# The first chunk's triangular inverse on VectorE instead of GpSimd, and the transfers of the first four chunks issued ahead of weight loads

## The chip, the cores and the metric

The kernel runs on one core of a Trainium2 chip. Its time is the device time of one execution in microseconds (us); the number that counts is the median of the runs. A core has five engines, each with an instruction queue of its own that runs in order: TensorE (PE in the profile, its weight loads PEld), VectorE (DVE), ScalarE (ACT), GpSimd (POOL) and SyncE (SP). SP and ACT also issue the DMA transfers here; a transfer that has to wait holds up everything behind it in its queue.

## What is computed

Three layers follow each other. The first is a linear recurrence over 768 time steps for 4 x 8 heads with a 40 x 40 state; the second and the third are feed-forward layers on the 3072 tokens that come out.

```python
for t in range(S):                                   # 768 steps
    y[:, :, t] = einsum('bhd,bhde->bhe', rt, state)
    Sa = einsum('bhde,bhe->bhd', state, at)
    state = state * wt[:, :, None, :] - einsum('bhd,bhe->bhde', Sa, bt) \
            + einsum('bhd,bhe->bhde', vt, kt)
...
h = x @ w_in;  x1 = (h - tanh(h)) @ w_out            # 3072 x 320, 2048 wide
...
out = sum over e of p[:, e] * (relu(x1 @ w1[e]) @ w2[e])   # 4 experts, 1024 wide
```

The weights of the second layer are 64-bit floating point numbers.

## The kernel before

**The recurrence in chunks.** Time is cut into chunks of 64 steps, and the batch into two halves, so there are 24 chunks, 12 for each half, each with 16 heads. Within a chunk the steps depend on each other through a lower triangular matrix, which is inverted in 32 x 32 blocks. A chunk goes through these stages, each a list of small steps:

- `pre`, first part (lines 262 to 277): the decay factors E are clamped and multiplied up by scans on VectorE, forward and back (L200), the keys KBT are scaled (L228), and zs is made from `a` (L217). It also issues the loads for the next chunk.
- `pre`, second part: TensorE makes the products M (L235). ScalarE copies one half of them to MB (L239), VectorE masks the other into zs (L242). `mb_out` writes MB to DRAM with four transfers in ScalarE's queue (L248). `back` turns the keys around (kbn, L257).
- `inverse` (L281 to L315): SP loads MB back as two tiles N (L288), spread so that the 128 partitions hold 16 heads' blocks, and an identity as Y (L291). Then follow 31 columns, j = 0 to 30, each with two GpSimd instructions: `tmp` is a column of Y times a row of N (L299), and Y is reduced by it (L301). Both read two tensors from SBUF and depend on the one before. SP stores Y to DRAM (L306) and reads it back as TT in another layout (L310).
- `chain` (L327): Z (L340) from the state, U = TT x Z for the first 32 steps (L349), R (L360), U for the second 32 steps, transposes T, and S, the new state. Chunk c + 1 cannot start its Z before S of chunk c.
- `post` (L408): the outputs of the chunk, SC on TensorE, which go to DRAM as xT (L441).

**Beside it: the weights of the second layer.** There are 32 blocks, up0, down0, up1 to down15. For each, SP loads a raw tile of 64-bit numbers (`raw_up`, `raw_down`, L492). The load waits for a one-element ScalarE copy from the block three before (`behind`, L174), so at most about three blocks are under way. ScalarE turns the high words into `t` (L454), VectorE decodes with four instructions (L455, L456, L458, L459), ScalarE rounds (L471), TensorE subtracts the rounded part with three matmuls ("rest", L478), and ScalarE keeps the remainder (L479). The second layer's blocks of 256 tokens (`moe1_all`) need all of that for their first round; its matmuls are "h" (L528, up) and "acc" (L591, down). Block 0 needs the outputs of chunks 0 and 1.

**What sets the order.** The steps are written in slots (`att_slot`, `spread`): slot i has the chain of chunk i, the end of the inverse of chunk i + 1, the start of that of chunk i + 2 (`INV_CUT` = 7 columns), the second part of `pre` for chunk i + 2, the first part for i + 3, and the outputs of chunk i - 1, mixed by share of the slot; weight blocks are spread over slots -0.5 to 1.75 (`share`), and the second layer begins with slot 2. A scheduler then reorders the instructions by its own estimate of when each can run, by the order of writing as priority. `soon(f)` raises a step's priority by `AHEAD` = 150 instructions. The result is one fixed order for each engine.

**Buffers.** N tiles are three: chunk c takes number 2c and 2c + 1 modulo 3, so chunk 0 has N0 and N1, chunk 1 N2 and N0, chunk 2 N1 and N2. Y and TT are two, by parity. `sc_r` is a pair of tiles that `post` uses; the first time is in chunk 0's outputs.

Of the kernel before, what the change touches and what calls it, by code (L numbers as in the profile page):

```python
# [11 lines left out]
F32 = mybir.dt.float32  # L12
# [29 lines left out]
def tile_wkv_then_moe_then_moe(ctx, tc, r, k, v, w, a, b, moe_w_in, moe_w_out, probs, w1, w2, wT, aT, rT, kbT, vP, vT, wi_in, wo_in, out):  # L42
    nc = tc.nc
# [7 lines left out]
    LAG = 1.25  # L51
    INV_CUT = 7
    AHEAD = 150
    RAW_AHEAD = 2
    CHECK_AT = 30
    NB = B // G
# [34 lines left out]
    ap2 = att.enter_context(tc.tile_pool(name="ap2", side="left", bufs=2))  # L91
# [18 lines left out]
    sc_r = [ap1.tile([128, HH // 2, C], F32, name=f"SC{i}") for i in range(2)]  # L110
# [65 lines left out]
    def soon(f):  # L176
        def g():
            with tc.high_priority(offset=AHEAD):
                f()
        return g  # L180
# [6 lines left out]
    def pre(hf, c, nxt, nxt_w):  # L187
# [57 lines left out]
        def mb_out(o):  # L245
            q = 64 * o
            for s in range(2):
                nc.scalar.dma_start(out=mt_d[c % 2][o, s].rearrange("h j t -> j h t"),  # L248
                                  in_=MB[q + 32 * s:q + 32 * s + 32, :, 32 * s:32 * s + 32])
# [16 lines left out]
        first = [clamp]  # L266
# [7 lines left out]
                first.append(lambda: [behind(zs[q:q + D, q // 64, 0, 0:1], e_r[nxt_w[1]][q:q + D, 0, 0:1]) for q in (0, 64)])  # L274
            first.append(lambda: load_w(*nxt_w, nc.scalar))
        second = [lambda g=g: m_step(g) for g in range(ng)]
        second += [lambda o=o: mb_out(o) for o in range(2)]
        second.append(back)
        return first, second

    def inverse(hf, c):  # L281
        N, Y, TT = [n_r[(2 * c + u) % 3] for u in range(2)], y_r[c % 2], tt_r[c % 2]
        X["TT", hf, c] = TT

        def load():
# [7 lines left out]
        def col(j):  # L293
            n = j // 4 + 1
            wd = 31 - j
            tmp = ap2.tile([128, 80], F32, tag="tmp", name="tmp", bufs=1)[:, 0:n * wd].rearrange("p (i t) -> p i t", i=n)
            u = j // 16
            nj = N[u][:, j - 16 * u:j - 16 * u + 1, j + 1:32]
            nc.gpsimd.tensor_tensor(out=tmp, in0=Y[:, 0:n, j:j + 1].to_broadcast([128, n, wd]),  # L299
                              in1=nj.to_broadcast([128, n, wd]), op=ALU.mult)  # L300
            nc.gpsimd.tensor_tensor(out=Y[:, 0:n, j + 1:32], in0=Y[:, 0:n, j + 1:32], in1=tmp,  # L301
                                    op=ALU.subtract)

        def store():
# [3 lines left out]
        def back():  # L308
            src = tt_d[c % 2][0]
            nc.sync.dma_start(out=TT.rearrange("p h t -> p (h t)"),  # L310
                              in_=bass.AP(src.tensor, src.offset, [[256, 4], [1024, 32], [1, 256]]))

        cols = [lambda j=j: col(j) for j in range(31)]
        return [load] + cols[:INV_CUT], cols[INV_CUT:] + [store, back]

    def start_half(hf):
        nc.gpsimd.memset(st, 0.0)
# [780 lines left out]
```

## Time and profile before

| | |
|---|---|
| median of 3 runs | 1610.53 us (1608.2 to 1612.03) |
| the profiled execution | 1613.03 us, span of its instructions 1611.3 us |
| TensorE busy | 1478.0 us, 92% of the span |
| VectorE | 807.2 us, 50% |
| ScalarE | 503.1 us, 31% |
| GpSimd | 586.7 us, 36% |
| mean granted TensorE clock | 0.948 of full speed |

The profile is one execution, taken by the hardware profiler, with the start and the duration of each instruction. An entry such as `N<-mt_d` names the output and the input of an instruction by the program's names. "Idle before" is the time in which the engine had nothing to run ahead of an instruction, and the arrow names what ended that. Rows of several like instructions are merged (x12), and the time is then the whole of them. The decode matmuls and the matmuls with 32-bit operands appear as more records than the program has instructions.

### The profile page before, as it was taken

What the parts mean: (1) busy time and instruction counts of PE and PEld (TensorE: products, weight loads), DVE (VectorE), ACT (ScalarE), POOL (GpSimd) and SP (SyncE); (2) the same over time, 40 slices, a digit from 0 to 9 for tenths busy, and PEclk for the clock granted to TensorE, in tenths of its full rate; (3) what the DMA queues carried; (4) which work ended last, traced back from release to release, by engine and by line L of the source; (5) the groups of instructions that cost most, each with busy time, mean ns of one, the idle gap of its engine ahead of it and who ended that gap; (6) DMA issues with size and microseconds to landing.
All of it is one profiled execution on the core that took longest, in us unless ns stands there. A gap on an engine that the chain in (4) does not pass through costs nothing.

```text
span 1611.3 us, 33016 instructions
## 1 busy us (share of the span) xinstructions
PE 1478.0 (92%) x13178; PEld 1330.4 (83%) x13178; DVE 807.2 (50%) x1604; ACT 503.1 (31%) x1239; POOL 586.7 (36%) x1543
## 2 busy tenths in 40 slices
PE   3587898898989899989998999999999999999998
PEld 2366698888878788879998989898898989898997
DVE  8588756665656566666556443332333333332332
ACT  3344433333333333333345462121221212121111
POOL 4888865648485484665703001000000101010000
PEclk9578799999998999999999999999999999999999
DMA  4556522332432323232215331000010101000011
GB/s 127 130 151 158 132 50 72 97 83 69 101 86 77 82 69 95 76 94 66 61 39 156 101 100 29 8 21 17 1 36 1 37 1 36 1 1 1 0 50 51
DMA packets 163938, 103.26 MB, mean 64 GB/s; under 512 B 101952, under 2 KB 139840, under 8 KB 163776
## 3 DMA queue, kind: packets, MB, share of 16 engines
q1 hardware_dynamic: 97412, 71.64, 16.1%
q10 hardware_dynamic: 66364, 29.44, 7.6%
q8 instruction: 105, 1.72, 0.4%
q14 instruction: 57, 0.47, 0.1%
HBM read 82.82 MB, written 18.22 MB: 63 GB/s over the span
## 4 chain that ended last, share of the span: by engine, by line
PE 57%; DMA 6%; POOL 5%; DVE 3%; issue 3%; ACT 1%; SPq 0%; ACTq 0%; DVEq 0%; POOLq 0%
PE h L528 26%; PE acc L1011 21%; PE acc L591 4%; POOL Y L301 2%; POOL tmp L299 2%; PE SC L418 1%; DMA E<-in_wT_dram 1%; DMA N<-mt_d 1%; DMA TT<-tt_d 1%; PE SC L429 1%; DMA tt_d<-Y 1%; PE SC L433 1%; PE M L235 1%; DMA KBT<-in_kbT_dram 1%; PE Z L340 1%
## 5 line engine op out<-in xcount | busy, mean ns | idle before, releaser
L299 POOL TENSOR_TENSOR tmp<-Y,N 128x60 f32<-128x60 f32 (+24 forms) x744 | 254.8, 343 | 208.3 <-DMA N<-mt_d 108.9
L998 DVE SCALAR_TENSOR_TENSOR hl<-h,hh 128x512 fp32r<-128x512 f32 x192 | 132.1, 689 | 332.9 <-ACT hh L997 332.8
L301 POOL TENSOR_TENSOR Y<-Y,tmp 128x60 f32<-128x60 f32 (+24 forms) x744 | 264.7, 356 | 58.3
L997 ACT ACTIVATE hh<-h 128x512 fp32r<-128x512 f32 x192 | 114.6, 598 | 505.2 <-PE h L528 505.1
L528 PE MATMUL h<-xh,up 128*128 128x256 f32 x1152 | 236.9, 301 | 24.3 <-DVE t L578 14.2
L1011 PE MATMUL acc<-w2h,hh 128*128 128x320 f32 x768 | 236.3, 308 | 0.6 <-DVE oacc L1016 0.6
L1011 PE MATMUL acc<-w2l,hh 128*128 128x320 f32 x768 | 236.4, 308 | 0.0
L1011 PE MATMUL acc<-w2h,hl 128*128 128x320 f32 x768 | 235.3, 308 | 0.2 <-DVE hl L998 0.2
L528 PE MATMUL h<-xh,w1h 128*128 128x512 f32 x576 | 227.8, 395 | 0.0
L528 PE MATMUL h<-xh,w1l 128*128 128x512 f32 x576 | 227.1, 394 | 0.0
L947 POOL TENSOR_TENSOR w1l<-w1r,w1h 128x1536 fp32r<-128x1536 f32 x8 | 28.0, 3498 | 528.4 <-ACT w1h L946 528.4
L528 PEld LDWEIGHTS h<-xh,up 128*128 128x128 f32 x1152 | 188.6, 201 | 31.4 <-DVE t L578 17.7
L591 PE MATMUL acc<-down,gh 128*128 128x320 f32 x768 | 171.3, 321 | 3.1 <-ACT gh L579 3.1
L1011 PEld LDWEIGHTS acc<-w2l,hh 128*128 128x128 f32 x768 | 144.0, 188 | 12.0
L1011 PEld LDWEIGHTS acc<-w2h,hh 128*128 128x128 f32 x768 | 144.1, 188 | 11.6 <-DVE oacc L1016 1.0
L528 PE MATMUL h<-xl,w1h 128*128 128x512 f32 x384 | 151.7, 395 | 0.0
L1011 PEld LDWEIGHTS acc<-w2h,hl 128*128 128x128 f32 x768 | 143.7, 187 | 0.7 <-DVE hl L998 0.5
L1018 DVE SCALAR_TENSOR_TENSOR oacc<-acc,pnorm,oacc 128x320 f32<-128x320 f32 x168 | 84.4, 544 | 116.2 <-PE acc L1011 116.2
L591 PEld LDWEIGHTS acc<-down,gh 128*128 128x128 f32 x768 | 124.3, 194 | 6.3 <-ACT gh L579 4.1
L577 ACT ACTIVATE t<-h 128x256 f32<-128x256 f32 x192 | 72.4, 384 | 180.9 <-PE h L528 110.6
L580 DVE TENSOR_TENSOR gl<-t,gh 128x256 fp32r<-128x256 f32 x192 | 93.4, 491 | 69.0 <-ACT gh L579 67.7
L591 PE MATMUL acc<-down,gl 128*128 128x320 f32 x384 | 113.5, 324 | 14.0 <-DVE gl L580 14.0
(138 smaller groups left out, 2317.6 us busy)
## 6 DMA issues: line engine op xcount, KB each, us to landing
N<-mt_d SPq DMA_DIRECT2D x48, 256.0 KB
KBT<-in_kbT_dram ACTq DMA_DIRECT2D x46, 160.0 KB
raw_up<-in_wi_dram SPq DMA_DIRECT2D x16, 384.0 KB
raw_down<-in_wo_dram SPq DMA_DIRECT2D x16, 320.0 KB
w2r<-in_moe_w_dram SPq DMA_DIRECT2D x8, 640.0 KB
w1r<-in_moe_w_dram SPq DMA_DIRECT2D x16, 256.0 KB
xT_d<-yT SPq DMA_DIRECT2D x48, 80.0 KB
wchk<-in_w_dram SPq DMA_DIRECT2D x5, 768.0 KB
```

Source lines behind the costliest of these rows:

```text
L235: nc.tensor.matmul(ps[:, 128 * j:128 * j + 128], KBT[:, p], zs[:, :, p], start=True, stop=True)
L299: nc.gpsimd.tensor_tensor(out=tmp, in0=Y[:, 0:n, j:j + 1].to_broadcast([128, n, wd]), in1=nj.to_broadcast([128, n, wd]), op=ALU.mult)
L301: nc.gpsimd.tensor_tensor(out=Y[:, 0:n, j + 1:32], in0=Y[:, 0:n, j + 1:32], in1=tmp, op=ALU.subtract)
L528: nc.tensor.matmul(ps, l, rr, start=(i == 0), stop=(i == len(ops) - 1))
L577: nc.scalar.activation(out=t, in_=ps, func=AF.Tanh)
L580: nc.vector.tensor_tensor(out=gl, in0=t, in1=gh, op=ALU.subtract)
L591: nc.tensor.matmul(M["acc"][tt], l[:, cs], rr, start=(f == 0 and i == 0), stop=(f == NF - 1 and i == 2))
L947: nc.gpsimd.tensor_tensor(out=w1l, in0=w1r, in1=w1h, op=ALU.subtract)
L997: nc.scalar.activation(out=hh_, in_=ps, func=AF.Relu)
L998: nc.vector.scalar_tensor_tensor(out=hl_, in0=ps, scalar=0.0, in1=hh_, op0=ALU.max, op1=ALU.subtract)
L1011: nc.tensor.matmul(po, l[:, cs], rr[:, f], start=(f == 0 and i == 0), stop=(f == FH - 1 and i == 2))
L1018: nc.vector.scalar_tensor_tensor(out=oacc[:, n], in0=po, scalar=pe, in1=oacc[:, n], op0=ALU.mult, op1=ALU.add)
```

## The change

Chunk 0's inverse is run by VectorE with a `tmp` tile of its own, chunk 1's stays on GpSimd. So that both can be under way, chunk 1's second N tile is no longer N0, which chunk 0 holds, but `sc_r[1]`. All steps of chunk 0's inverse are written with `soon`; so are, for the first four chunks of the first half, the write of MB, the load of N, and the store and read-back of the result.

```diff
+    FIRST_INV = (0,)
...
         second = [lambda g=g: m_step(g) for g in range(ng)]
-        second += [lambda o=o: mb_out(o) for o in range(2)]
+        second += [(soon if hf == 0 and c < 4 else lambda f: f)(lambda o=o: mb_out(o)) for o in range(2)]
         second.append(back)
...
         N, Y, TT = [n_r[(2 * c + u) % 3] for u in range(2)], y_r[c % 2], tt_r[c % 2]
+        first = hf == 0 and c in FIRST_INV
+        eng, tag = (nc.vector, "tmpv") if first else (nc.gpsimd, "tmp")
+        if (hf, c) == (0, 1):
+            N[1] = sc_r[1].rearrange("p a (b t) -> p (a b) t", b=2)
...
-            tmp = ap2.tile([128, 80], F32, tag="tmp", name="tmp", bufs=1)[:, 0:n * wd].rearrange("p (i t) -> p i t", i=n)
+            tmp = ap2.tile([128, 80], F32, tag=tag, name="tmp", bufs=1)[:, 0:n * wd].rearrange("p (i t) -> p i t", i=n)
...
-            nc.gpsimd.tensor_tensor(out=tmp, in0=Y[:, 0:n, j:j + 1].to_broadcast([128, n, wd]),
+            eng.tensor_tensor(out=tmp, in0=Y[:, 0:n, j:j + 1].to_broadcast([128, n, wd]),
...
-            nc.gpsimd.tensor_tensor(out=Y[:, 0:n, j + 1:32], in0=Y[:, 0:n, j + 1:32], in1=tmp,
+            eng.tensor_tensor(out=Y[:, 0:n, j + 1:32], in0=Y[:, 0:n, j + 1:32], in1=tmp,
...
-        return [load] + cols[:INV_CUT], cols[INV_CUT:] + [store, back]
+        head, tail = [load] + cols[:INV_CUT], cols[INV_CUT:] + [store, back]
+        if first:
+            return [soon(f) for f in head], [soon(f) for f in tail]
+        if hf == 0 and c < 4:
+            return [soon(load)] + head[1:], tail[:-2] + [soon(store), soon(back)]
+        return head, tail
```

VectorE has 61 rows more in the new order, GpSimd 62 less. The line numbers of the changed kernel are higher: L299 and L301 become L304 and L306, and what stands behind `inverse` moves by 10. Three places show how the queues changed.

The first is VectorE's queue around chunk 0's first U (`vu0_93<-U_761` is its copy out of PSUM; `t0`, `t1` and `f2` belong to the decode, whose fourth instruction for a block names the raw tile, and `E4` to the first part of chunk 4). Before:

```order
L456 SCALAR_TENSOR_TENSOR t0_639<-t0_639,t1_640 128x384
L200 SCALAR_TENSOR_TENSOR E4_119<-E4_119,start_103 128x260 x2
L458 TENSOR_SCALAR t1_640<-t0_639 128x384
L353 TENSOR_SCALAR vu0_93<-U_761 32x8x40
L459 SCALAR_TENSOR_TENSOR f2_641<-raw_up4_567,t1_640 128x384
L455 TENSOR_SCALAR t1_676<-t0_675 128x320
L456 SCALAR_TENSOR_TENSOR t0_675<-t0_675,t1_676 128x320
```

and now:

```order
L465 TENSOR_SCALAR t1_980<-t0_979 128x320
L466 SCALAR_TENSOR_TENSOR t0_979<-t0_979,t1_980 128x320
L468 TENSOR_SCALAR t1_980<-t0_979 128x320
L363 TENSOR_SCALAR vu0_93<-U_761 32x8x40
L469 SCALAR_TENSOR_TENSOR f2_981<-raw_down8_901,t1_980 128x320
L465 TENSOR_SCALAR t1_1003<-t0_1002 128x384
L374 TENSOR_TENSOR Z_590<-R_852,Z_590 32x320 x2
```

The copy of U stood behind the third decode instruction of block up4, the ninth of 32, and now stands behind that of down8, the eighteenth.

The second place is the same queue at the end of chunk 0's inverse, whose rows are L304 and L306 and which was not there before:

```order
L304 TENSOR_TENSOR tmp_488<-Y0_123,N1_121 128x24
L468 TENSOR_SCALAR t1_836<-t0_835 128x320
L306 TENSOR_TENSOR Y0_123<-Y0_123,tmp_488 128x8x3
L469 SCALAR_TENSOR_TENSOR f2_837<-raw_down6_740,t1_836 128x320
L304 TENSOR_TENSOR tmp_509<-Y0_123,N1_121 128x16
L465 TENSOR_SCALAR t1_880<-t0_879 128x384
L306 TENSOR_TENSOR Y0_123<-Y0_123,tmp_509 128x8x2
L466 SCALAR_TENSOR_TENSOR t0_879<-t0_879,t1_880 128x384
L304 TENSOR_TENSOR tmp_513<-Y0_123,N1_121 128x8
L468 TENSOR_SCALAR t1_880<-t0_879 128x384
L306 TENSOR_TENSOR Y0_123<-Y0_123,tmp_513 128x8
L469 SCALAR_TENSOR_TENSOR f2_881<-raw_up7_785,t1_880 128x384
```

Between the last columns stand the decode of blocks down6 and up7; in the same way the earlier columns stand between the decode of the blocks from up1 on, the fourth decode instruction of down0, and the first parts of chunks 2, 3 and 4 (of chunk 4 the clamp and the scans). The inverse's first row comes behind the first mask of chunk 1's M, the last one here.

The third place is SP's queue around the stores of the inverses (`tt_d0<-Y0` is chunk 0's, `tt_d1<-Y1` chunk 1's; the `N1` load is half of chunk 2's). Before:

```order
L492 DMA raw_down3_529<-in_wo_dram 128x320
L492 DMA raw_up4_567<-in_wi_dram 128x384
L288 DMA N1_121<-mt_d0_59 128x1x512
L306 DMA tt_d0_61<-Y0_123 128x8x32
L492 DMA raw_down4_599<-in_wo_dram 128x320
L310 DMA TT0_125<-tt_d0_61 128x1x256
L291 DMA Y0_123<-eye_d_63 128x256
L492 DMA raw_up5_636<-in_wi_dram 128x384
```

and now, where the loads of up6, down6 and up7 stand at the "...":

```order
L311 DMA tt_d1_62<-Y1_124 128x8x32
L502 DMA raw_down5_672<-in_wo_dram 128x320
L315 DMA TT1_126<-tt_d1_62 128x1x256
L296 DMA Y1_124<-eye_d_63 128x256
L502 DMA raw_up6_714<-in_wi_dram 128x384
...
L502 DMA raw_up8_876<-in_wi_dram 128x384
L293 DMA N1_121<-mt_d0_59 128x1x512
L311 DMA tt_d0_61<-Y0_123 128x8x32
L502 DMA raw_down8_901<-in_wo_dram 128x320
L315 DMA TT0_125<-tt_d0_61 128x1x256
L296 DMA Y0_123<-eye_d_63 128x256
```

Chunk 1's store has moved ahead of chunk 0's; chunk 0's store, the read-back and the identity for chunk 2 have moved from ahead of up5's load to behind up8's.

On TensorE, 49 of the 96 decode matmuls now stand ahead of chunk 0's first U (22 before), 94 ahead of chunk 3's Z (67 before), and the first "h" stands just ahead of chunk 3's Z (before: behind the R of chunk 4). Ahead of chunk 4's Z there are 104 h and 60 acc (none before), ahead of chunk 5's Z 128 and 81 (64 and 36 before), ahead of chunk 6's Z 184 and 126 in both.

## Rows read from the trace of the kernel before

**Rows 1.** Stretches: busy PE, PEld, DVE, ACT, POOL; clock, DMA share, GB/s.

```profile
33.00:109.00 76.00, 51.66 (x483) 35.69 (x483) 53.37 (x113) 32.54 (x92) 63.46 (x161) 0.64 0.53 137
...
198.00:270.00 72.00, 64.57 (x650) 59.99 (x652) 43.35 (x93) 27.05 (x77) 49.03 (x144) 0.91 0.26 61
...
270.00:860.00 590.00, 541.85 (x6968) 503.45 (x6967) 355.46 (x757) 212.52 (x614) 334.65 (x996) 0.95 0.31 79
```

**Rows 2.** Order of time, GpSimd's columns, one VectorE row: start, duration, engine, line.

```profile
33.01 0.40 POOL L299 TENSOR_TENSOR tmp<-Y,N 128x31 f32<-128x31 f32 x1 [18.23 <-DMA N<-mt_d]
...
63.94 0.36 POOL L301 TENSOR_TENSOR Y<-Y,tmp 128x8 f32<-128x8 f32 x1
...
91.35 0.21 POOL L301 TENSOR_TENSOR Y<-Y,tmp 128x8 f32<-128x8 f32 x1
...
97.31 1.98 POOL L299 TENSOR_TENSOR tmp<-Y,N 128x48 f32<-128x48 f32 x1
...
97.55 1.21 DVE L217 TENSOR_TENSOR zs<-aT,E 128x1024 f32<-128x1024 f32 x1
```

**Rows 3.** Order of time, SP's queue: chunk 0's store and read-back.

```profile
64.48 0.47 SPq L306 DMA_DIRECT2D tt_d<-Y  x1
...
70.16 0.54 SPq L310 DMA_DIRECT2D TT<-tt_d  x1
```

**Rows 4.** Order of time, TensorE: U and Z of chunks, and h.

```profile
74.53 0.61 PE L349 MATMUL U<-Z,TT 32*32 32x40 f32 x12 [7.61 <-DMA TT<-tt_d]
...
95.61 1.13 PE L340 MATMUL Z<-vu,zs 104*64 104x40 f32 x32
...
101.26 0.47 PE L349 MATMUL U<-Z,TT 32*32 32x40 f32 x14
...
146.65 1.93 PE L340 MATMUL Z<-vu,zs 104*64 104x40 f32 x32 [0.25 <-DVE vu L379]
...
187.56 0.51 PE L349 MATMUL U<-Z,TT 32*32 32x40 f32 x18 [0.48 <-DMA TT<-tt_d]
...
198.64 0.39 PE L528 MATMUL h<-xh,up 128*128 128x256 f32 x1 [2.46 <-ACT down L479]
...
219.67 0.39 PE L528 MATMUL h<-xh,up 128*128 128x256 f32 x1
...
221.93 0.39 PE L528 MATMUL h<-xh,up 128*128 128x256 f32 x1
...
226.35 0.78 PE L340 MATMUL Z<-vu,zs 104*64 104x40 f32 x20
...
235.27 0.76 PE L349 MATMUL U<-Z,TT 32*32 32x40 f32 x32
...
269.81 1.13 PE L340 MATMUL Z<-vu,zs 104*64 104x40 f32 x32
```

**Rows 5.** Groups on VectorE, 33 to 109 us: busy, mean ns, idle before.

```profile
L217 DVE TENSOR_TENSOR zs<-aT,E 128x1024 f32<-128x1024 f32 x3 | 3.7, 1249 | 0.0
...
L435 DVE TENSOR_TENSOR yT<-SC,E 128x256 f32<-128x256 f32 x2 | 0.8, 424 | 0.3 <-PE SC L433 0.3
...
L455 DVE TENSOR_SCALAR t<-t 128x384 int32<-128x384 int32 x8 | 2.9, 360 | 0.4
...
L456 DVE SCALAR_TENSOR_TENSOR t<-t,t 128x384 int32<-128x384 int32 x8 | 4.5, 557 | 0.2
...
L459 DVE SCALAR_TENSOR_TENSOR f<-raw_up,t 128x384 fp32r<-128x384 uint32 x7 | 4.0, 573 | 0.2
...
L200 DVE TENSOR_TENSOR_SCAN E<-E,start 128x260 f32<-128x260 f32 x6 | 4.1, 720 | 0.0
...
L228 DVE TENSOR_TENSOR KBT<-KBT,RW 128x512 f32<-128x512 f32 x6 | 4.3, 750 | 0.1
...
L242 DVE TENSOR_TENSOR zs<-M,mask 64x256 f32<-64x256 f32 x8 | 3.4, 422 | 2.7 <-ACT MB L239 2.6
...
L263 DVE TENSOR_SCALAR E<-E 128x512 f32<-128x512 f32 x3 | 1.4, 468 | 8.3 <-DMA E<-in_wT_dram 8.3
```

## The prediction, made before the changed kernel was run

> **What bounds the kernel now.** I read two views in this order. First the busy times by stretch [rows 1]: from 33 to 109 us TensorE is busy 51.7 of 76 us at a granted clock of 0.64, from 198 to 270 us 64.6 of 72, from 270 to 860 us 541.9 of 590. From about 200 us on TensorE is the bound; before that it waits, so what there is to gain lies in the first 200 us. Then the order of time on GpSimd and on TensorE, to see for what. GpSimd starts chunk 0's inverse at 33.01 us, when the tiles N have landed (its idle time before is put down to that transfer), and ends it at 64.30 (63.94 + 0.36); it goes on without a gap to 91.56 with chunk 1 [rows 2], 27.3 us later, and so on. Each inverse is stored to DRAM and read back as TT [rows 3]; TensorE's first product with it (U) starts at 74.53, after a wait of 7.61 us for TT, so 10.2 us after GpSimd's last column [rows 4]. The U of chunk 1 follows at 101.26, of chunk 4 at 187.56; the matmuls of the first MoE (h) run on from 198.64, after a wait of 2.46 us for the last weight block [rows 4]. So two ladders run beside each other until 200 us: inverses on GpSimd, 27 to 31 us a chunk, and the decode of 32 weight blocks on VectorE, ScalarE and TensorE.
>
> **What is moved, and what that costs.** The idea is plain: with chunk 0 on VectorE and chunk 1 on GpSimd at the same time, GpSimd is one inverse ahead, at most 27.3 us. But a queue runs in order, and the order decides. On VectorE the 62 instructions of chunk 0's inverse don't stand in a block: the decode of the weights stands between them, from the end of block 1 (down0) to block 14 (up7), and beside it the whole first part of chunks 2 and 3, and most of chunk 4's. So chunk 0's inverse ends only when VectorE has done all of that too.
>
> *The 62 instructions.* The trace shows no such instruction on VectorE. Nearest rows: 128x1024 takes 1249 ns, 128x256 takes 424 ns [rows 5], which gives 1.07 ns an element and a fixed 149 ns. The inverse has 1,560 elements a partition in each of its two kinds of instruction, 50 on average: 62 x 149 + 3,120 x 1.07 = 12.6 us, with some 40 ns between instructions 15 us. The lower bound is the line through the two rows without gaps, 12.6 us; the upper one GpSimd's own 31.3 us for the same chunk [rows 2]. I take 15 us, since both rows are of the same engine and type.
>
> *The work between them.* A decoded "up" block costs VectorE 360 + 557 + 360 + 573 ns = 1.85 us (the third instruction is of the first one's kind) [rows 5]; 12 blocks and most of two more, half of them a sixth narrower: 23 us. The first part of a chunk is two pairs of scans of 720 ns, a pair of KBT products of 750 ns, zs with 1249 ns, a clamp with 468 ns and 0.4 us of small things [rows 5]: 6.5 us, for chunks 2 and 3 13 us, for chunk 4 without KBT and zs 3.8 us. Eight masks at 422 ns [rows 5]: 3.4 us. Together 43 us, gaps included. Of this nothing is new, but in the kernel before it didn't stand ahead of the inverse.
>
> *Waits among them.* From 33 to 109 us VectorE is idle for 76 - 53.4 = 22.6 us [rows 1], 8.3 of them for the transfers of E [rows 5]. With 15 us more work in the gaps most of that is covered; I leave 6 us. So chunk 0's inverse ends at 33 + 15 + 43 + 6 = **97 us**, where GpSimd had it at 64.3. Bounds: 89 without waits, about 120 with the upper price for the 62.
>
> *Chunk 0's chain.* U starts 10.2 us after, at 107 (74.5 before).
>
> *Chunk 1 and 2 on GpSimd.* N of chunk 1 can land by about 45 us (its source is written to DRAM behind a ScalarE instruction that waits for chunk 0's N, so from 33 us; I allow 12 us for the write and the read, where store and read-back of TT took 10.2), so chunk 1 is ready at about 72 and waits for chunk 0. Chunk 2 uses the Y and one N of chunk 0: its loads stand behind chunk 0's store on SP, so it starts about 8 us after 97 (store 64.48, next 70.16, then the transfer [rows 3]), at 105 instead of 91.6, and chunk 3 ends at 105 + 2 x 28 = 161 instead of 152. GpSimd's ladder is therefore later, not earlier; but TT of chunk 3, at 161 + 10 = 171, comes before it is needed (below).
>
> *What is gained in exchange.* The decode is ahead: in the order of TensorE 49 of its 96 decode matmuls stand ahead of chunk 0's U (22 before), 94 ahead of chunk 3's Z (67 before). Between chunk 0's U and chunk 3's Z there are 45 in both. So this stretch took 146.65 - 74.53 = 72.1 us before [rows 4] and should take a little less, since TT of chunk 1 and 2 no longer ends last: the Z of chunk 1 is there at 95.61, its U only at 101.26 [rows 4], some 3 of those 5.7 us a wait. I take 67 (57 to 74: at the lower end each of the three steps loses 5 us of waits for raw weights and E too). Chunk 3's Z is then at 107 + 67 = **174 us**, and with it the first MoE begins, which ran on from 198.64 before, when chunks 3 and 4 had their U behind them.
>
> *From there to a common state.* At chunk 6's Z both orders have the same 184 "h" and 126 "acc" matmuls behind them; before, that is at 269.81 [rows 4]. Eight h and six acc and two Z take 221.93 - 219.67 = 2.26 us [rows 4]. After: Z to U of chunk 3 5 us; U of chunk 3 to Z of chunk 4 with 88 h and 60 acc 35 us (187.56 to 226.35 and its 0.8 us is 39 us for 88 h, 54 acc, five decode matmuls and two waits [rows 4]); 3 us to U; then 24 h and 21 acc (6.5 us) and the chain of a chunk (11 us) to Z of chunk 5, 18 us; 3 us to U; and 56 h and 45 acc with a chain 26 us (34.5 us for 72 and 60 from 235.27 to 269.81, with a wait for x [rows 4]). Sum 90 us: 174 + 90 = 264, against 269.8. **Gain 5.6 us**, within 1 and 12 by the 57 to 74 us and the 6 us of waits. Beyond 270 us TensorE is busy 92% in both, so a lead stays. The other transfers that are issued earlier (MB out, N, store and back of chunks 1 to 3) cost nothing of their own: none of these chunks' inverses is what ends last any more.
>
> The profiled execution took 1613.0 us (span 1611.3), the median is 1610.5. On the median: 1610.5 - 5.6 = **1605 us**.
>
> **Rivals.** *A. Two vector engines in each other's way: slower.* GpSimd's 128x48 product at 97.31 took 1.98 us while VectorE ran zs from 97.55 on, an instruction of two SBUF inputs; the other columns of that group take 0.21 to 0.40 [rows 2]. Place: chunk 1's inverse on GpSimd, now beside a VectorE that hardly pauses. Its store stands on SP ahead of raw_down5 and, with the wait for TT, of raw_up6 to raw_up8, and VectorE's last inverse columns stand behind the decode of just those blocks. If chunk 1 ends at t, the blocks land and are decoded by about t + 14 (5.7 us from store to next issue [rows 3], some 5 us for the transfer, 3 us of VectorE). It decides from t = 88, when chunk 0's inverse passes 102.6 and the gain is gone: 16 us on 62 instructions, 0.26 us each. With 0.4 us each t is 97, the inverse ends at 111, 14 us later than in the forecast, and the time is 1605 + 14 = 1619. For it: the row at 97.31. Against: the first two inverses ran beside a VectorE that was busy for 70% of the time and took 31.3 and 27.3 us [rows 1, 2]. The Trainium skill, "GPSIMD Engine Reference", section "Key points", says that GpSimd shares its SBUF interfaces with VectorE and contends with instructions of two SBUF inputs, which all of the moved ones are; by that rule this rival would be the likely one, and the row at 97.31 agrees in kind.
>
> *B. The full step: much faster.* The decode blocks arrive so early that VectorE runs without a wait and at the lower price, the inverse ends at 85 to 88, and the early chain loses its waits too: gain 5.6 + 10 + 7 = 22 us, 1588. Against it: the 43 us of other work are in the order whatever happens.
>
> *C. Nothing left at the end.* The lead at chunk 6 is lost behind it, because the order of all later instructions is a new one: 1610. The time of 270 to 860 us has 48 us of TensorE idle [rows 1], in which a few us can come or go.
>
> **Chances.** Forecast 0.45 (0.32 of it a gain over 3.2 us, which is 0.2% and about what a measurement of this kernel tells from no change), A 0.27 (0.25 slower by more), B 0.17, C 0.11. That is faster 0.49, same 0.26, slower 0.25. The range reaches to most of B and A: 1589 to 1620.
>
> **What would show it.** In the trace after: the last 128x8 column of the inverse on VectorE at 97 us (89 to 105); the first U near 107; GpSimd's second inverse starting after 100, not at 72; the first h between 165 and 180; chunk 6's Z near 264. Wrong if VectorE's inverse ends by 85 (B), if chunk 1's ends after 88 on GpSimd (A), or if chunk 6's Z is early and the end is not (C).

## The result: 1.0% slower

| | before | after |
|---|---|---|
| median of 4 runs each | 1609.37 us (1606.28 to 1612.03) | 1627.6 us (1621.26 to 1629.46) |
| ratio | | 1.0101, 95% interval 1.0076 to 1.0126 |
| span of the profiled execution | 1611.3 us | 1627.7 us |
| first U | 74.5 us | 104.3 us |
| chunk 6's Z | 269.8 us | 277.0 us |
| from there to the end | 1341.5 us | 1350.7 us |

Of the 16.4 us between the two profiles 7.2 are lost up to chunk 6's Z, the point at which both orders have the same work behind them, and 9.2 behind it.

The busy times of the changed kernel by stretch (columns as in [rows 1]), cut at its first U, chunk 3's Z and chunk 6's Z:

```profile
33.00:104.30 71.30, 35.37 (x110) 19.92 (x112) 52.53 (x160) 27.89 (x82) 27.12 (x62) 0.60 0.51 135
104.30:179.00 74.70, 64.60 (x800) 48.88 (x801) 59.49 (x126) 35.16 (x95) 50.81 (x138) 0.77 0.51 134
179.00:277.00 98.00, 90.30 (x1112) 82.08 (x1110) 61.62 (x131) 33.27 (x96) 69.98 (x208) 0.91 0.32 84
33.00:277.00 244.00, 190.27 (x2016) 150.87 (x2016) 173.65 (x416) 96.33 (x273) 147.91 (x407) 0.78 0.44 114
277.00:1627.70 1350.70, 1279.30 (x11095) 1170.86 (x11094) 616.56 (x1211) 395.34 (x938) 395.94 (x1042) 0.97 0.20 53
```

The same stretches of the kernel before, cut at its own three points:

```profile
33.00:74.50 41.50, 18.48 (x72) 10.95 (x73) 27.25 (x58) 14.97 (x47) 34.84 (x86) 0.58 0.57 143
74.50:146.70 72.20, 61.75 (x798) 47.47 (x798) 57.71 (x122) 35.41 (x96) 60.21 (x154) 0.78 0.57 149
146.70:269.80 123.10, 106.25 (x1146) 92.73 (x1146) 80.27 (x172) 47.73 (x131) 91.40 (x258) 0.84 0.36 91
33.00:269.80 236.80, 186.48 (x2014) 151.15 (x2014) 165.23 (x351) 98.10 (x274) 186.45 (x496) 0.78 0.46 118
269.80:1611.30 1341.50, 1280.35 (x11095) 1169.81 (x11094) 615.86 (x1210) 395.03 (x937) 386.58 (x1014) 0.98 0.20 53
```

Length less TensorE's busy time is its idle time. Up to the first U it is 35.9 us (23.0 before), from there to chunk 6's Z 17.8 (27.3 before), behind that 71.4 (61.1 before). So of the 13 us of idling that the later U adds, 9.5 are earned back by chunk 6. Behind it all the loss is idle time.

The steps of the early part, in order of time on VectorE, GpSimd, SP and TensorE (they answer to [rows 2 to 4]):

```profile
33.73 0.19 DVE L304 TENSOR_TENSOR tmp<-Y,N 128x31 f32<-128x31 f32 x1 [6.56 <-DMA N<-mt_d]
45.06 0.20 DVE L304 TENSOR_TENSOR tmp<-Y,N 128x50 f32<-128x50 f32 x1
52.35 0.31 DVE L304 TENSOR_TENSOR tmp<-Y,N 128x48 f32<-128x48 f32 x1
93.20 0.17 DVE L306 TENSOR_TENSOR Y<-Y,tmp 128x8 f32<-128x8 f32 x1
...
46.91 0.24 POOL L304 TENSOR_TENSOR tmp<-Y,N 128x31 f32<-128x31 f32 x1 [32.15 <-DMA N<-mt_d]
78.42 0.39 POOL L306 TENSOR_TENSOR Y<-Y,tmp 128x8 f32<-128x8 f32 x1
104.51 0.24 POOL L304 TENSOR_TENSOR tmp<-Y,N 128x31 f32<-128x31 f32 x1 [25.70 <-DMA Y<-eye_d]
144.92 0.29 POOL L304 TENSOR_TENSOR tmp<-Y,N 128x31 f32<-128x31 f32 x1 [13.01 <-DMA N<-mt_d]
...
94.00 0.42 SPq L311 DMA_DIRECT2D tt_d<-Y  x1
100.11 0.56 SPq L315 DMA_DIRECT2D TT<-tt_d  x1
...
104.27 1.27 PE L359 MATMUL U<-Z,TT 32*32 32x40 f32 x32 [4.53 <-DMA TT<-tt_d]
171.84 0.38 PE L538 MATMUL h<-xh,up 128*128 128x256 f32 x1 [1.44 <-ACT up L489]
276.97 1.13 PE L350 MATMUL Z<-vu,zs 104*64 104x40 f32 x32
```

VectorE's inverse runs from 33.7 to 93.4 us, though its own 62 instructions need 14.6 us of that; the rest is decode and first parts of chunks between them. GpSimd runs chunk 1 from 46.9 to 78.8, then has nothing to do for 25.7 us. The inverse's two groups on VectorE, 33 to 93.4 us, and that of the first decode instruction, which bears the longest waits:

```profile
L304 DVE TENSOR_TENSOR tmp<-Y,N 128x60 f32<-128x60 f32 (+24 forms) x31 | 7.4, 240 | 6.7 <-DMA N<-mt_d 6.6
L306 DVE TENSOR_TENSOR Y<-Y,tmp 128x60 f32<-128x60 f32 (+24 forms) x31 | 7.1, 230 | 0.1
L465 DVE TENSOR_SCALAR t<-t 128x384 int32<-128x384 int32 (+1 forms) x13 | 4.5, 343 | 11.0 <-ACT t L464 11.0
```

The largest new stall behind chunk 6 is at chunk 11's Z. Order of time on TensorE and ScalarE there:

```profile
438.50 1.79 PE L350 MATMUL Z<-vu,zs 104*64 104x40 f32 x29 [7.64 <-issue]
...
425.52 0.60 ACTq L171 DMA_DIRECT2D vu<-in_vP_dram  x1
435.89 0.59 ACTq L171 DMA_DIRECT2D vu<-in_vP_dram  x1
436.58 0.38 ACT L587 ACTIVATE t<-h 128x256 f32<-128x256 f32 x1 [9.96 <-DMA N<-mt_d]
```

and ScalarE's waits there (total, times, longest):

```profile
ACT t L587 <- DMA N<-mt_d: 10.0, 1, 10.0
```

Two loads of vu, which otherwise follow each other by 0.7 us, stand 10.4 us apart: ScalarE, which issues them, is held at the second until a load of N from SP's queue has landed, and with it all ScalarE work behind. The order of ScalarE's queue shows what the second one waits for:

```
507 L171 DMA vu1_94<-in_vP_dram 64x8x40 [waits DMAHW3_49,PE_49]
508 L615 ACTIVATE x1T_4384<-x1T_4380 128x256 [waits PE_49]
509 L616 ACTIVATE x1T_4384<-x1T_4380 64x128
510 L171 DMA vu1_94<-in_vP_dram 64x8x40 [waits DMAHW4_49]
```

In the listing the transfers of SP and ScalarE take turns on eight counters, DMAHW0 to 7, and each issue waits for an earlier transfer on its counter. Which transfers meet on one counter, and whether TensorE has other work just then, depends on the order, and the change makes a new order for the whole first layer.

### The profile page after: what moved, and what is told of

Read it like the earlier page. It is cut to its first block, busy times and chain, and to the rows that moved or that the text cites. A ratio compares the mean times of both kernels' runs of the same rounds, so it can differ in the third digit from the quotient of the medians.

```text
span 1627.7 us, 33015 instructions
## 1 busy us (share of the span) xinstructions
PE 1480.7 (91%) x13178; PEld 1331.1 (82%) x13178; DVE 814.1 (50%) x1666; ACT 501.6 (31%) x1239; POOL 557.5 (34%) x1481
## 4 chain that ended last, share of the span: by engine, by line
PE 62%; DMA 4%; DVE 2%; ACT 0%; issue 0%; SPq 0%; ACTq 0%; DVEq 0%
PE h L538 28%; PE acc L1021 21%; PE acc L601 6%; PE SC L428 1%; DMA E<-in_wT_dram 1%; PE SC L439 1%; PE SC L443 1%; PE M L236 1%; DMA KBT<-in_kbT_dram 1%; DMA TT<-tt_d 1%; PE U L359 1%; PE Z L350 1%; DMA N<-mt_d 1%; DVE gl L590 1%; DMA w2r<-in_moe_w_dram 0%; PE R L370 0%
## 5 line engine op out<-in xcount | busy, mean ns | idle before, releaser
L304 POOL TENSOR_TENSOR tmp<-Y,N 128x60 f32<-128x60 f32 (+24 forms) x698 | 236.7, 339 | 259.0 <-DMA N<-mt_d 106.0
L306 POOL TENSOR_TENSOR Y<-Y,tmp 128x60 f32<-128x60 f32 (+24 forms) x713 | 246.7, 346 | 55.8
L538 PEld LDWEIGHTS h<-xh,w1l 128*128 128x128 f32 x576 | 108.3, 188 | 21.8
```

Source lines behind the costliest of these rows:

```text
L304: eng.tensor_tensor(out=tmp, in0=Y[:, 0:n, j:j + 1].to_broadcast([128, n, wd]), in1=nj.to_broadcast([128, n, wd]), op=ALU.mult)
L306: eng.tensor_tensor(out=Y[:, 0:n, j + 1:32], in0=Y[:, 0:n, j + 1:32], in1=tmp, op=ALU.subtract)
L538: nc.tensor.matmul(ps, l, rr, start=(i == 0), stop=(i == len(ops) - 1))
```

## The experiments

Chunk 6's Z divides every run in two, since its order on each variant has 184 h, 126 acc and all 96 decode matmuls ahead of it, but for e11 (176 and 118) and e18 (192 and 127). U and Z are starts in us; "behind" is from chunk 6's Z to the end of the span, "idle" TensorE's idle time in it; the ratio is to the kernel before, run beside it. U, Z, "behind" and "idle" are of the one profiled execution of each variant; the ratios rest on all its runs (two of e10 and e18, four to ten of the others).

| | first U | chunk 6's Z | behind | idle | ratio, 95% interval |
|---|---|---|---|---|---|
| before | 74.5 | 269.8 | 1341.5 | 61 | 1 |
| after | 104.3 | 277.0 | 1350.7 | 71 | 1.0101 (1.0076 to 1.0126) |
| e1 transfers only | 76.4 | 266.2 | 1356.7 | 64 | 1.0031 (1.0013 to 1.0048) |
| e2 inverse only | 96.7 | 282.2 | 1355.8 | 72 | 1.0147 (1.0114 to 1.0179) |
| e3 chunk 1 on VectorE | 74.3 | 274.7 | 1344.1 | 60 | 1.0046 (1.0024 to 1.0067) |
| e4 after, 0.44 | 102.5 | 273.6 | 1356.2 | 75 | 1.0091 (1.0061 to 1.0121) |
| e5 before, 0.44 | 73.5 | 267.4 | 1361.2 | 81 | 1.0107 (1.0068 to 1.0147) |
| e6 before, vu on SP | 72.6 | 266.9 | 1338.9 | 60 | 0.9986 (0.9970 to 1.0002) |
| e7 after, 0.36 | 103.5 | 273.2 | 1342.6 | 73 | 1.0048 (1.0031 to 1.0065) |
| e8 after, vu on SP | 104.4 | 273.2 | 1354.4 | 71 | 1.0096 (1.0062 to 1.0130) |
| e9 inverse 0 left out | 59.4 | 271.0 | 1345.4 | 64 | 1.0020 (0.9997 to 1.0042) |
| e10 no second N | 105.7 | 290.3 | 1349.3 | 70 | 1.0176 (1.0125 to 1.0228) |
| e11 decode later | 95.2 | 280.2 | 1347.2 | 67 | 1.0102 (1.0064 to 1.0140) |
| e12 before, 0.36 | 74.4 | 272.7 | 1345.5 | 65 | 1.0032 (1.0014 to 1.0051) |
| e13 before, half columns | 55.8 | 272.0 | 1350.0 | 66 | 1.0061 (1.0034 to 1.0089) |
| e14 before, light decode | 72.3 | 259.0 | 1357.8 | 71 | 1.0003 (0.9988 to 1.0017) |
| e15 before, 0.42 | 74.1 | 273.1 | 1361.6 | 75 | 1.0092 (1.0071 to 1.0114) |
| e16 after, 0.42 | 103.5 | 274.4 | 1365.4 | 76 | 1.0146 (1.0113 to 1.0179) |
| e17 before, one twin | 77.6 | 264.7 | 1341.1 | 67 | 0.9983 (0.9959 to 1.0008) |
| e18 before, three twins | 77.7 | 291.3 | 1350.7 | 70 | 1.0200 (1.0131 to 1.0269) |

Five profiles share the early order of the kernel before (before, e5, e6, e12, e15): chunk 6's Z at 266.9 to 273.1, mean 270.0. Five share that of the changed one (after, e4, e7, e8, e16): 273.2 to 277.0, mean 274.3. So one profile is good to some 3 us there (e4, e7 and e8 came out 3 us under the changed kernel's 277.0, in the same order), and the early loss is 4.3 us rather than 7.2.

### The parts of the change: e1, e2, e3

```diff
e1  -    FIRST_INV = (0,)
    +    FIRST_INV = ()
e2  -        second += [(soon if hf == 0 and c < 4 else lambda f: f)(lambda o=o: mb_out(o)) for o in range(2)]
    +        second += [lambda o=o: mb_out(o) for o in range(2)]
    -        if hf == 0 and c < 4:
    -            return [soon(load)] + head[1:], tail[:-2] + [soon(store), soon(back)]
e3  -    FIRST_INV = (0,)
    +    FIRST_INV = (1,)
```

> All inverses stay on GpSimd; the transfers of the first four chunks are still written with priority, and chunk 1 has its own second N tile. Three theories. T1 (early loss comes from chunk 0's inverse standing between decode instructions on VectorE; the loss behind chunk 6 is a matter of the order of the later queues): first U at 74 to 78 us, chunk 6's Z at 266 to 273 (269.8 before, 277.0 in the changed kernel); what lies behind it anywhere between 1338 and 1355 us (1341.5 before, 1350.7 changed). T2 (the transfers moved ahead of the weight loads delay the decode): chunk 6's Z at 274 or later. T3 (the loss behind chunk 6 is carried over from the early one): with chunk 6's Z back near 270 the rest is back at 1340 to 1343.

> Chunk 0's inverse on VectorE as in the changed kernel; the transfers of chunks 1 to 3 and all four writes of MB have the priority of the kernel before. T1: VectorE's last inverse column ends at 90 to 96 us, first U at 101 to 107, chunk 6's Z at 274 to 280, and the part behind it differs from that of the changed kernel (1350.7 us) by several us in either direction, since the later order is another one. T2: chunk 6's Z back at 269 to 272. T3: with chunk 6's Z near 277 the part behind it is 1349 to 1352 again.

> Chunk 1's inverse goes to VectorE and chunk 0's stays on GpSimd; all else as changed. T1: the first U is back at 74 to 77 us, since chunk 0's inverse has GpSimd's queue to itself; chunk 1's inverse ends on VectorE between 85 and 100 us, which its Z (95.6 before) hardly notices; GpSimd starts chunk 2 at 68 to 80 us instead of 91.6 and is then ahead for good. Chunk 6's Z at 262 to 268. The time is 3 to 8 us under the kernel before if the part behind chunk 6 stays as before, within 10 of that otherwise. Rival (two vector engines in each other's way): chunk 0's inverse ends on GpSimd after 68 us instead of 64.3, first U after 79, and chunk 6's Z is not before 270.

T2 falls: with the transfers alone chunk 6's Z is at 266.2, and without them at 282.2 (2 us above T1's range as well). The early loss comes with chunk 0's inverse on VectorE. T3 falls with e1 (early part restored, the rest longer) and with e2. Of the 15.2 us by which e1's rest is longer, though, 12.7 are TensorE's busy time (1293.0 us at a mean granted clock of 0.96, against 1280.3 at 0.98 before), and e1's profiled execution took 4.3 us more than the median of its ten. But e3 went against T1: the first U is early, GpSimd starts chunk 2 at 74.7, and still chunk 6's Z is at 274.7. GpSimd then stood idle for 15.5 us at 103 and again waited for N: a ladder that gets ahead waits for its input.

### Only the order behind chunk 6: e4, e5, e7, e12, e15, e16

```diff
-        return [(cat(P, "chain"), 0, 1), (iv + cat(P, "head"), 0, 1), (cat(P, "post"), 0, POST_END),
+        return [(cat(P, "chain"), 0, 1), (iv + cat(P, "head"), 0, 1), (cat(P, "post"), 0, POST_END if i < 7 else 0.44),
```

(0.36 in e7 and e12, 0.42 in e15 and e16.)

> The changed kernel with another mixing of the later slots (outputs of a chunk spread to 0.44 of a slot instead of 0.40, from slot 7 on): nothing that stands ahead of chunk 6's Z is touched. T1: chunk 6's Z at 276 to 278 as in the changed kernel, and the part behind it is moved by 3 us or more from 1350.7, so that this part is a matter of order. T3: the part behind it stays within 2 us of 1350.7.

> The kernel before with the other mixing of the later slots (0.44 instead of 0.40 from slot 7 on); nothing ahead of chunk 6's Z is touched. Measure: TensorE's idle time behind chunk 6's Z, 61 us in the kernel before, 71 in the changed one, 63, 72, 59 and 74 in the four runs so far. T1 (that time is a matter of the order of the later queues, and the kernel before had a good one): it grows to 66 us or more and the kernel is 4 to 14 us slower than before. T3 (it is bound to where chunk 0's inverse runs: 59 to 63 us with it on GpSimd, 71 to 74 on VectorE): it stays at 59 to 63 us and the time within 3 us of before.

> The changed kernel with a third mixing of the later slots (0.36 from slot 7 on). T1: TensorE's idle time behind chunk 6's Z is anywhere between 58 and 76 us. T3: 69 to 75 us once more. Both: chunk 6's Z at 273 to 278 us, as the order ahead of it is the same.

> The kernel before with a third mixing of the later slots (0.36 from slot 7 on). Chunk 6's Z at 266 to 270 us. T1 (the order of the later queues alone moves the rest): TensorE's idle time behind chunk 6's Z anywhere between 58 and 82 us (61 in the kernel before, 81 with 0.44), and the time between 1.000 and 1.011 of the kernel before.

> The kernel before with a fourth mixing of the later slots (0.42 from slot 7 on). If the order of the later queues alone makes the time behind chunk 6: 1338 to 1362 us there (1341.5, 1361, 1345.5 for 0.40, 0.44, 0.36), ratio to before 1.000 to 1.012.

> The changed kernel with the same fourth mixing (0.42 from slot 7 on). If the order alone makes the time behind chunk 6: 1340 to 1360 us there, and over the four mixings the mean of the changed kernel lies above that of the kernel before by no more than the 5 us that are lost up to chunk 6, give or take 5. If the change itself costs behind chunk 6 as well: the mean is above by 12 us or more, with TensorE idle there for 70 us or more again.

This settles that the order behind chunk 6 can cost as much by itself. With not one instruction touched ahead of it, the kernel before becomes 1.07% slower (e5; 4 to 14 us had been expected, it is 17), as much as by the whole change. Its idle time behind chunk 6 rises to 81 us, here its largest stall (order of time, TensorE):

```profile
562.58 0.69 PE L390 MATMUL T<-ident,vu 64*128 64x64 f32 x8 [10.83 <-DVE vu L353]
```

Over the four mixings (0.40, 0.44, 0.36, 0.42) the part behind takes 1341.5, 1361.2, 1345.5 and 1361.6 us in the kernel before, mean 1352.5, and 1350.7, 1356.2, 1342.6 and 1365.4 in the changed one, mean 1353.7. (e16's 1365.4 lies above the 1340 to 1360 expected.) These figures are of one execution each, and not all of their differences is idle time: with the same instructions TensorE is busy for 1269.7 us in e7, whose profiled execution took 4.0 us less than the median of its eight, and for 1289.1 in e16. What the order does is clearest in e5, whose 19.7 us more are idle time alone, and in the ratios, which rest on all runs. The ratios average 1.0058 and 1.0097: the change costs 0.39%, 6 us, with a standard error of about 5 from their scatter, so four orders can't tell it from nothing. At 0.44 the changed kernel is not even the slower one. The kernel before stood on the best of its four orders.

### Where ScalarE's transfers stand: e6, e8

```diff
-                ps.insert(2, lambda: load_v(*hc[i + 1], nc.scalar))
+                ps.insert(2, lambda: load_v(*hc[i + 1], nc.scalar if i < 6 else nc.sync))
```

> The kernel before with the loads of v (vu) from chunk 7 on issued from SP's queue instead of ScalarE's; nothing ahead of chunk 6's Z is touched. Theory T4 (TensorE's stalls behind chunk 6 come from ScalarE held by a transfer's issue that waits for another transfer, above all by the second vu load): the waits of ScalarE's t for a transfer of SP (N, tt_d, TT: 17 us in two before) become less, and TensorE's idle time behind chunk 6's Z falls from 61 to 52 to 58 us. Rival (SP is then held in turn, and N or TT comes late): U waits for TT appear and the idle time is 61 us or more.

> The changed kernel with the loads of vu from chunk 7 on issued from SP's queue. T4: the stalls at chunk 11's Z (7.6 us) and in chunk 16 (5.6 us), in which ScalarE stood at the second vu load until N had landed, are gone; TensorE's idle time behind chunk 6's Z falls from 71 to 55 to 62 us, and the time by 8 to 14 us against the changed kernel. T3: it stays near 71 us, the stalls only move.

T4 falls as a remedy. In e6 the idle time is 60 us (52 to 58 expected, 61 before), and the interval of the ratio reaches to 1. The stall at chunk 11's Z is gone in e8, but others come (4.8 us at chunk 12's R, 4.4 at an acc in chunk 8), the one at chunk 12's second U stays (6.3 us, 6.5 in the changed kernel), and the idle time stays at 71. The one stall was read rightly; the sum of them isn't that queue's.

### What binds the time up to chunk 6: e9, e13, e14

```diff
e9   -        cols = [lambda j=j: col(j) for j in range(31)]
     +        cols = [lambda j=j: col(j) if j == 0 or not first else None for j in range(31)]
e13  -        cols = [lambda j=j: col(j) for j in range(31)]
     +        cols = [lambda j=j: col(j) if j % 2 == 0 or hf or c > 6 else None for j in range(31)]
e14  -        nc.vector.tensor_scalar(out=t2, in0=t1, scalar1=3, scalar2=None, op0=ALU.logical_shift_left)
     -        nc.vector.scalar_tensor_tensor(out=t1, in0=t1, scalar=-0x80000000, in1=t2, op0=ALU.bitwise_and,
     -                                       op1=ALU.bitwise_or)
```

> The changed kernel without columns 1 to 30 of chunk 0's inverse (only its first column is computed, so chunk 0's result is not the recurrence's). It shows what the early part would be if that inverse were free. T1 (the inverse's late end on VectorE is what costs the time up to chunk 6): the first U at 45 to 55 us, and chunk 6's Z at 250 to 260 (268 to 270 in the kernel before, 273 to 277 changed). T5 (the early part is bound by TensorE's own work and the decode that feeds it, and where the first U stands hardly matters): the first U just as early, but chunk 6's Z still at 262 to 270.

> The kernel before with every second column left out of the inverses of chunks 0 to 6 (their results are not the recurrence's), so that each step of GpSimd's ladder takes about 14 us instead of 27 to 31. Theory L (the ladder of inverses binds the first 270 us): chunk 6's Z falls from 267 to 273 (four executions of that order) to 240 to 258. T5 (TensorE's work and the decode that feeds it bind it): chunk 6's Z stays at 263 to 273, although chunk 3's inverse ends some 60 us earlier.

> The kernel before without the first two of the four decode instructions on VectorE (the weights of the second layer are then wrong): some 0.9 us less for each of 32 blocks, 29 us of VectorE's work before the last block. T5a (VectorE's share of the decode binds the early part): chunk 6's Z falls to 245 to 258. T5b (TensorE with its waits for ScalarE and for raw blocks binds it): chunk 6's Z stays at 261 to 272.

The ladder of inverses doesn't bind (theory L falls, T5 holds). In e13, order of time on GpSimd, the end of chunk 2's inverse and the start of chunk 3's:

```profile
81.67 0.29 POOL L301 TENSOR_TENSOR Y<-Y,tmp 128x8 f32<-128x8 f32 x1
103.68 0.24 POOL L299 TENSOR_TENSOR tmp<-Y,N 128x31 f32<-128x31 f32 x1 [21.72 <-issue]
```

Chunk 2's inverse ends 38 us earlier than before (120.3), yet chunk 3's Z is at 147.2 (146.7 before) and chunk 6's Z at 272.0. (Chunk 3's own inverse ends 32 us earlier, at 119.7, not 60 as expected, since GpSimd waited 21.7 us ahead of it.) In e9 chunk 0's inverse is free, and that gives nothing against the kernel before: chunk 6's Z is at 271.0, far from T1's 250 to 260 and 1 us above T5's range. Busy times from 33 us to chunk 6's Z, of e9, e13 and e14 (columns as above):

```profile
33.00:271.00 238.00, 186.55 (x2014) 151.43 (x2014) 167.73 (x355) 96.67 (x272) 161.04 (x431) 0.80 0.46 118
```

```profile
33.00:272.04 239.04, 185.41 (x2014) 152.00 (x2012) 159.06 (x340) 95.65 (x271) 106.24 (x283) 0.80 0.46 117
```

```profile
33.00:258.99 225.99, 179.56 (x2010) 147.53 (x2010) 137.48 (x283) 95.18 (x270) 174.20 (x493) 0.82 0.48 123
```

In e13 GpSimd works 80 us less than before, and TensorE's busy and idle times (185 and 54 us) are those of before (186 and 50). Only less VectorE work (e14, 28 us less) brings chunk 6's Z down, by 11 us against the mean of 270.0. That lies between the ranges of T5a and T5b. Half of the 11 us are busy time (179.6 us, 185.0 on the mean of the five profiles of that order) at a mean granted clock of 0.82 (0.76 to 0.78 in those), half idle time (46.4 us, 52.0). So VectorE's decode is likely a part of what binds, not all; one execution doesn't show it. The end gained nothing of it: in the order of e14 the part behind takes 1357.8 us.

### Less overlap, later decode: e10, e11

```diff
e10  -        if (hf, c) == (0, 1):
     -            N[1] = sc_r[1].rearrange("p a (b t) -> p (a b) t", b=2)
e11  -    DEC_FROM = -0.5
     +    DEC_FROM = 0.0
```

> The changed kernel without the second N tile for chunk 1: its N1 is N0 again, which chunk 0 holds, so GpSimd's inverse of chunk 1 can't run beside VectorE's of chunk 0. Theory T6 (the two engines slow each other): all of VectorE's 62 inverse instructions take 0.16 to 0.22 us (up to 0.34 in the changed kernel from 52 to 75 us), their sum falls from 14.5 to about 12 us, and GpSimd's chunk 1 takes 27 to 28 us instead of 31.9. T1: the end of VectorE's inverse moves by those 2 to 3 us only, to 89 to 92. Both: GpSimd starts chunk 1 only at 70 or later (N0 is free when column 15 is done), and if it ends after 115 the U of chunk 1 waits for it.

> The changed kernel with the weight decode written from slot 0 on instead of from slot -0.5 on, so that 44 instead of 58 decode instructions stand ahead of the last inverse column on VectorE. T1: that column ends at 80 to 88 us instead of 93.4, the first U at 90 to 98. If what costs is the late first U, chunk 6's Z comes 3 to 8 us earlier, at 266 to 272. T5 (TensorE's work, fed by the decode, is the bound): the decode is later by as much, chunk 6's Z at 273 to 282.

e10 didn't keep the engines apart: chunk 1's first N tile was free, so its first 16 columns ran on GpSimd from 46 us, beside VectorE. It tells nothing of T6. VectorE's inverse ended at 94.3 (89 to 92 expected). It shows the price of an in-order queue, though, at the end of VectorE's inverse (order of time):

```profile
87.87 0.17 DVE L302 TENSOR_TENSOR tmp<-Y,N 128x8 f32<-128x8 f32 x1
93.85 0.36 DVE L463 TENSOR_SCALAR t<-t 128x384 int32<-128x384 int32 x1 [5.81 <-ACT t L462]
94.12 0.17 DVE L304 TENSOR_TENSOR Y<-Y,tmp 128x8 f32<-128x8 f32 x1
```

The very last instruction of the inverse, 0.17 us long, stands 6 us behind a decode instruction that waits for its weights. In e11 the inverse ends at 84.1 and the first U comes at 95.2, but chunk 6's Z at 280.2: the decode that was put off costs more than the earlier U gives.

### VectorE's work without the late inverse: e17, e18

```diff
+        def twin(j):
+            n = (j // 4 + 1) * (31 - j)
+            tv = ap2.tile([128, 80], F32, tag="tmpv", name="tv", bufs=1)[:, 0:n]
+            nc.vector.tensor_tensor(out=tv, in0=N[0][:, 0, 0:n] if j == 0 else ident[:, 0:n], in1=ident[:, 0:n], op=ALU.mult)
+            nc.vector.tensor_tensor(out=tv, in0=tv, in1=ident[:, 0:n], op=ALU.subtract)
...
-        cols = [lambda j=j: col(j) for j in range(31)]
+        cols = [lambda j=j: (col(j), soon(lambda: twin(j))()) if hf == 0 and c < 1 else col(j) for j in range(31)]
```

(c < 3 in e18.)

> The kernel before, in which VectorE runs a twin of chunk 0's inverse beside GpSimd: 62 instructions of the same sizes on constants, from the landing of N on, whose results nobody uses. Chunk 0's inverse itself stays on GpSimd, so the first U should stay at 72 to 80 us. W (VectorE's added work is what costs up to chunk 6; by the lighter decode, 11 us for 29, some 0.4 us for each): chunk 6's Z at 273 to 278 (before 266.9 to 273.1 in five executions, mean 270.0; changed kernel 273.2 to 277.0, mean 274.3). Rival (the late end of chunk 0's inverse is what costs): 266 to 272 as before.

> The same with twins of the inverses of chunks 0, 1 and 2: 186 instructions, some 44 us more work for VectorE. (192 h and 127 acc stand ahead of chunk 6's Z here, 8 and 1 more than elsewhere, some 2 us.) W: chunk 6's Z at 282 to 294. Rival: 268 to 276.

W is not borne out for the amount that the change adds. VectorE's groups of the twin in e17:

```profile
L307 DVE TENSOR_TENSOR tv<-ident 128x60 f32<-128x60 f32 (+23 forms) x30 | 8.7, 291 | 0.3
L308 DVE TENSOR_TENSOR tv<-tv,ident 128x60 f32<-128x60 f32 (+24 forms) x31 | 8.3, 268 | 0.3
```

and, in order of time, GpSimd's first and last column of chunk 0:

```profile
30.99 0.24 POOL L299 TENSOR_TENSOR tmp<-Y,N 128x31 f32<-128x31 f32 x1 [14.80 <-DMA N<-mt_d]
66.45 0.37 POOL L301 TENSOR_TENSOR Y<-Y,tmp 128x8 f32<-128x8 f32 x1
```

17 us more on VectorE, and GpSimd's chunk 0 slowed from 31.3 to 35.8 us, move the first U by 3 us and cost nothing by chunk 6 (264.7, even below the rival's 266 to 272) nor at the end (0.9983, an interval that reaches to 1). That the added work is free is not shown by this, though. Up to chunk 6 (columns as in [rows 1])

```profile
33.00:264.68 231.68, 177.80 (x2014) 143.64 (x2013) 176.65 (x411) 95.97 (x272) 189.99 (x492) 0.82 0.47 120
```

the mean granted clock of this execution was 0.82 and TensorE busy for 177.8 us, 7 less than on the mean of the five profiles of the kernel before; its idle time of 53.9 us is 2 us above theirs. Three times that amount does cost (291.3, with 67.0 us idle). All four orders with the first U at 95 us or later have chunk 6's Z at 273 or later (after, e2, e10, e11). With the first U at 56 to 78 it lies at 259 to 275, e18 with its 48 us of added work apart. So the early loss is found with the late U; but all four of these orders also run chunk 0's inverse on VectorE, and e10 and e11 differ in more than that, so that the late U is its cause is not shown. An early U gains nothing, and the 4 us of the changed kernel are no more than other orders of the same work differ by.

## Why the prediction was wrong, step by step

**VectorE's queue was read rightly.** The 62 instructions took 14.6 us (15 forecast), the inverse ended at 93.4 (97), the first U came at 104.3 (107), GpSimd's second inverse started at 104.5 (105). In part that is luck: VectorE's waits between were 11.0 us for ScalarE's t alone, where 6 were allowed for all, and the durations of neighbouring instructions overlap by 9 us, where 40 ns were added between two. The work between, 42 us by its durations, was sized right (43). The Trainium skill, "VectorE: DVE Perf Modes", section "The TRN2 errata — SBUF-src ops pay a fixed extra latency per instruction", gives (N + 151) / 0.96 ns for an fp32 tensor_tensor of N elements and calls it exact at 512 and 2048; carried down to these sizes it makes an estimated 13.0 us for the 62. The trace agrees with it while GpSimd is idle (0.17 us for 8 elements, 0.20 for 50), beside GpSimd's inverse it doesn't (0.31 us for 48).

**Chunk 1 and rival A.** Chunk 1 took 31.9 us on GpSimd instead of 27, so the two engines do slow each other, as e17 shows by itself. A's row at 97.31 was no exception: in the kernel before five of the 62 instructions of chunk 0's inverse take 0.66 to 1.59 us, each beside zs, KBT or a mask on VectorE, so that some of this price was in the 31.3 us already. But chunk 1 ended at 78.8, well under the 88 us from which A would decide. Chunk 3's inverse ended at 172.9 instead of 161, since its N was loaded behind chunk 2's store and read-back; no U waited for it.

**First U to chunk 3's Z: 67 us forecast (57 to 74), 74.7 measured.** This step failed. It took 5 us off the 72.1 of the kernel before for waits for TT that would come back. But TensorE has no wait for TT in that stretch: its wait of 7.61 us lies ahead of the first U, and the U at 101.26 [rows 4] follows other matmuls without a gap. The largest waits there are for other things (kernel before, order of time):

```profile
118.22 2.08 PE L418 MATMUL SC<-rd,VUT 128*128 128x128 f32 x8 [2.94 <-ACT VUT L398]
144.46 0.43 PE L429 MATMUL SC<-rd,S 128*64 128x128 f32 x2 [2.18 <-DVE SC L420]
```

So nothing could come back there: TensorE's idle time in the stretch is 10.1 us now and 10.4 before, and its busy time 2.9 us longer. The sum also put nothing for the first four h, which the new order has ahead of chunk 3's Z. The first waits 1.44 us for a weight block (171.84, above), the second for the tokens:

```profile
175.12 0.58 PE L538 MATMUL h<-xl,up 128*128 128x256 f32 x1 [2.90 <-DVE xl L578]
```

In the four other profiles of that order the waits of these four are 3.5 to 6.6 us. e9 and e13 show without the change that inverses that are there earlier don't bring chunk 3's Z forward: it is at 145.3 and 147.2 (146.7 before).

**Chunk 3's Z to chunk 6's Z: 90 us forecast, 98.0 measured**, 94 to 96 in the four other profiles of that order. From Z to Z the three steps take 37.5, 22.1 and 38.3 us (40, 21 and 29 forecast; 38 to 40, 23 to 24 and 31 to 34 in the others). What was mis-sized in all five are the 3 us from Z to U, in chunk 4 (4.8 us) and chunk 5 (9.2 us, 5.4 to 6.5 in the others): between them TensorE's queue has the SC and M of other chunks. The rest of the 38.3 us is of this execution, at a mean granted clock of 0.82 in that step (0.90 to 0.95 in the others).

**"Beyond 270 us TensorE is busy 92% in both, so a lead stays": false**, and the largest miss, 9.2 us. From 270 to 860 us TensorE is busy for 531.1 us in the changed kernel, 90%. Rival C named the new order, but only as a lead that melts away. The eight orders of the two kernels spread the part behind chunk 6 from 1341.5 to 1365.4 us, several times the 5.6 us that I expected to gain ahead of it, and the kernel before stood on the best of its four. Together the misses are 7.7 + 8.0 + 9.2 us, less 2.7 by which the first U was early: 22.2 of the 22.6 us between 1605 and 1627.6. A change that reorders everything draws a new one: that belonged into the range, on the side of a loss above all.

**What stays open.** Why the same work up to chunk 6 takes 4 us longer with the late first U: idle time is 53 us on the mean of the five profiles (52 before; 50.4 to 54.5 and 50.3 to 55.6, so not told apart), busy time 188 (185), and the granted clock (0.77 to 0.80, and 0.76 to 0.78 before) doesn't explain it. Whether the change costs anything of its own behind chunk 6 is not told apart from the scatter of the orders.

## What to carry to other kernels

Before costing what a freed engine gains, shorten that engine's work in a throwaway kernel: here half of GpSimd's ladder could go without moving the end of the stretch. In an in-order queue a chain of short dependent instructions lasts as long as all that the scheduler puts between them (14.6 us became 60). And where a scheduler reorders the whole program, compare several orders of both versions: a single pair said 1.0%, four pairs 0.4% with a standard error of nearly as much.

## What had not been expected of the hardware

- Small VectorE instructions with two SBUF inputs take 0.16 to 0.21 us while GpSimd is idle and up to 0.34 beside GpSimd's inverse; the first chunk's inverse takes 31.3 us on GpSimd in the kernel before and 35.8 beside a twin on VectorE.
- A transfer's issue held ScalarE for 9.96 us until an unrelated transfer on the same counter, the load of N in SP's queue, had landed.
- The same order gives chunk 6's Z within 6 us from one execution to another (266.9 to 273.1), and the same kernel times within 0.8% (1607.1 to 1619.4 us over 20 runs of the kernel before on one chip).
